# The last group of a two-level Winograd projection: another product is taken plainly and comes last

## The chip, the cores and the metric

The kernel runs on one core of a Trainium2 chip. Its time is the device time of one execution in microseconds (us); several executions are made, and the median counts. A profile is one further execution, recorded instruction by instruction. The engines of the core are named as the profile names them: PE is TensorE (matrix products; PEld is its loading of weights), DVE is VectorE (elementwise arithmetic), ACT is ScalarE (here copies, squares, and one of the two queues from which transfers are issued), POOL is GpSimd, and SP is SyncE, which issues most transfers. PSUM is the memory that TensorE writes its products into; it is taken in banks of 128 partitions by 512 fp32 numbers. All else on the chip lies in SBUF.

## The reference

An attention block without softmax, then a feed-forward block with two matrices multiplied element by element:

```python
kv  = np.einsum('bhsd,bhse->bhde', k, v)          # q, k, v: (8, 8, 576, 64)
out = np.einsum('bhsd,bhde->bhse', q, kv)
rms = np.sqrt(np.mean(out * out, axis=-1, keepdims=True) + 1e-06)
x   = (out / rms * g_norm)                        # turned to (4608, 512)
a = x @ w1                                        # w1, w2: (512, 1024)
b = x @ w2
h = a * b @ w3                                    # w3: (1024, 1024)
return (h @ w_out)                                # w_out: (1024, 512)
```

All is fp32. The weights come as 64-bit floats and are converted in the kernel.

## The kernel before, in words

**Folding.** `w3 @ w_out` is computed once, at the start, into `w3o_sb` (1024 by 512, held as 128 partitions x 8 chunks x 512). What is left of the feed-forward block is then `(x w1) * (x w2)`, and that times `w3o`.

**Groups.** The 4608 rows are worked on in nine groups of 512 rows. Eight are the first 512 rows of a batch each; the ninth collects the 64 rows that are left over of every batch. The order is 0 to 6, then the left-over rows, then batch 7. In a group, `gates` computes `ab = (x w1) * (x w2)` in four pieces `p`, and then the projection multiplies `ab` by `w3o`. Attention for the next batch is threaded between the pieces; the last two groups have none of it.

**Winograd products.** A product of two 2x2 block matrices A and B is made of seven block products instead of eight (Winograd's form of Strassen's algorithm). With sums s1, s2, s3, s4 of A's blocks and differences t1, t2, t3, t4 of B's blocks, the products are

- p1 = a11 b11, a12 b21, p5 = s1 t1, s2 t2, s4 b22, s3 t3, a22 t4;
- u2 = p1 + s2 t2, u3 = u2 + s3 t3;
- c11 = p1 + a12 b21, c12 = u2 + p5 + s4 b22, c22 = u3 + p5, c21 = u3 + a22 t4.

The sums over several products are partly made in PSUM (a product is added onto a bank that holds an earlier one), partly by VectorE out of a copy kept in SBUF.

**Two levels.** The projection of the first group uses this once (`project`). That of the other eight groups (`project_twice`) uses it twice: each of the seven block products ("sets" here) is itself made of seven products of a quarter of the size. The sets are numbered by what they multiply: 0 is a11 b11, 1 is s1 t1, 2 is s2 t2, 3 is s4 b22, 4 is s3 t3, 5 is a12 b21, 6 is a22 t4. For a set n,

- `sum_inner(n)` makes the inner sums of the A side on VectorE: four additions of 128x256, three into one of three buffers (`inner_sums[n % 3]`), and the last in place in the block itself;
- `load_b()` fetches the B side of the next set, made ready beforehand, from device memory into one of three stream buffers, on SP's queue or, for sets 3 and 5, on ScalarE's;
- `products(n, ps)` runs the seven small products (L898) into two PSUM banks, four in the first and three in the second; given banks `ps` of an earlier set it adds onto them, unless `new` is true, when the banks are begun afresh;
- `keep(name, ps)` copies both banks to SBUF on ScalarE (L909, L910), and `add(z, ps)` adds them onto such a copy on VectorE (L937, L938), one instruction a bank;
- `finish(z, half, j)` combines the seven parts of a block of the result and writes it to `o_sbs[half]`, four instructions (L919 to L922). For the last group it also stores the block (`store_block`), except where the block still lacks a term.

A block (half, j) is the result's c(half+1)(j+1): rows of one half, columns of one half.

**The last group** (`last`) doesn't run set 6. Its product a22 t4 is taken plainly instead, in `last_block`: eight matmuls of 128x256 (two halves `m` of the rows, four chunks) into one bank, the two halves side by side. VectorE then adds each half onto block (1,0), which `finish(z, 1, 0)` has left without that term, and two stores bring it out, one on SP's queue and one on ScalarE's. A matmul in fp32 leaves two records in the trace, so that a set of fourteen matmuls has 28 and the plain product 16.

**Preparing the B side.** `prepare_b`, threaded through the second group, makes the inner differences of the seven B blocks (in place for one of them) and writes all to `w3o_l2` in device memory: parts 0 to 6. Before any of it, it saves one block untransformed as part 7: this is what the plain product multiplies by. `load_b` reads part `n % 7` for the n-th load; the last load of all, `ALL_B - 1`, reads the first 1024 columns of part 7.

**Order.** TensorE's, POOL's and SP's instructions are issued in the order in which the program makes them; VectorE's too within `project_twice` (a manual schedule, L1123). Where a later instruction would write what an earlier one reads, or the other way round, a semaphore keeps them apart.

Of the kernel before, what the change touches and what calls it, by code (L numbers as in the profile page):

```python
# [21 lines left out]
def kernel(  # L22
# [32 lines left out]
    nc = tc.nc  # L55
    PSUM = bass.MemoryType.PSUM
    P = 128
# [24 lines left out]
    def bank(pool, tag):  # L82
        return pool.tile([P, 512], FP32, name=tag, tag=tag)
# [717 lines left out]
    def prepare_b():  # L801

        nc.sync.dma_start(
            out=w3o_l2[7, :, 0:1024].rearrange("p (f n) -> p f n", n=N), in_=b_blocks()[6]
        )
        for n, y in enumerate(b_blocks()):
            b11, b12, b21, b22 = (
                y[:, 2 * i:2 * i + 2, j * P:(j + 1) * P] for i in range(2) for j in range(2)
            )


            stage = w3o_sums[0].rearrange("p f n -> p (f n)") if n == 4 else (
                o_sbs[(n - n // 5) % 2].rearrange("p m n -> p (m n)")
            )
            stage = stage[:, 0:6 * P]
            t1, t2, t4 = (t.rearrange("p (c n) -> p c n", n=P) for t in (
                stage[:, i * 2 * P:(i + 1) * 2 * P] for i in range(3)
            ))
            nc.vector.tensor_sub(t1, b12, b11)
            nc.vector.tensor_sub(t2, b22, t1)  # L820
            nc.vector.tensor_sub(b12, b22, b12)
            nc.vector.tensor_sub(t4, b21, t2)
            nc.sync.dma_start(
                out=w3o_l2[n, :, 0:1024].rearrange("p (f n) -> p f n", n=N), in_=y
            )
            nc.sync.dma_start(out=w3o_l2[n, :, 1024:PART], in_=stage)
            yield
# [4 lines left out]
    def load_b():  # L832
        n = len(loaded_b)
        if n == ALL_B:
            return
        t = streams[n % len(streams)]

        queue = nc.scalar if n % 7 in (3, 5) else nc.sync
        if n + 1 < ALL_B:
            queue.dma_start(out=t, in_=w3o_l2[n % 7])  # L840
        else:
            t = t[:, 0:1024]
            queue.dma_start(out=t, in_=w3o_l2[7, :, 0:1024])
        loaded_b.append(t)

    inner = {}

    def sum_inner(n, between=lambda: None):

        s1, s2, s4 = ab_sums  # L850
        x = [ab[0][:, :, 0], s1, s2, s4, ab[0][:, :, 1], ab[1][:, :, 0], ab[1][:, :, 1]][n]
        a11, a12, a21, a22 = (
            x[:, 2 * j:2 * j + 2, i * P:(i + 1) * P] for i in range(2) for j in range(2)
        )
        s1, s2, s4 = inner_sums[n % 3]
        nc.vector.tensor_add(s1, a21, a22)
        nc.vector.tensor_sub(s2, s1, a11)
        nc.vector.tensor_sub(s4, a12, s2)
        between()
        nc.vector.tensor_sub(a21, a11, a21)  # L860
        inner[n] = [a11, a12, a22, s1, s2, s4, a21]

    def project_twice(T, last, ahead):
        def store(half):
            if T < B:
                rows = out[T * S:T * S + G, :].rearrange("(p j) f -> p j f", j=J)
                nc.sync.dma_start(out=rows[:, 2 * half:2 * half + 2, :], in_=o_sbs[half])
                return
            for m in range(2):
                for l in range(2):  # L870
                    b = 2 * (2 * half + m) + l
                    nc.sync.dma_start(
                        out=out[b * S + G:(b + 1) * S, :], in_=o_sbs[half][l * L:(l + 1) * L, m, :]
                    )

        def products(n, ps=None):

            new = ps is None or n == 5
            if ps is None:
                ps = [bank(ps_mm, "mm").rearrange("p (i n) -> p i n", n=P) for _ in range(2)]  # L880
            a11, a12, a22, s1, s2, s4, s3 = inner[n]
            w = loaded_b[7 * done[T] + n]
            b = w[:, 0:1024].rearrange("p (f n) -> p f n", n=N)
            b11, t3, b21, b22 = (
                b[:, 2 * i:2 * i + 2, j * P:(j + 1) * P] for i in range(2) for j in range(2)
            )
            t1, t2, t4 = (
                w[:, 1024 + 256 * i:1280 + 256 * i].rearrange("p (c n) -> p c n", n=P)
                for i in range(3)
            )  # L890
            seen = set()
            for place, x, y in (
                (0, a11, b11), (3, a12, b21), (1, a22, t4), (2, s1, t1), (6, s2, t2), (5, s4, b22),
                (4, s3, t3),
            ):
                to, i = ps[place // 4], place % 4
                for c in range(2):
                    nc.tensor.matmul(  # L898
                        to[:, i, :], lhsT=x[:, c, :], rhs=y[:, c, :],
                        start=new and place // 4 not in seen,  # L900
                        stop=(c == 1),
                        skip_group_check=True,
                    )
                    seen.add(place // 4)
            return ps

        def keep(name, ps):
            t = late_tile(name)
            nc.scalar.copy(t[:, 0:4], ps[0])  # L909
            nc.scalar.copy(t[:, 4:7], ps[1][:, 0:3])  # L910
            return t

        def finish(z, half, j):

            def wide(i):
                return z[:, i:i + 1].to_broadcast([P, 2, P])

            dst = o_sbs[half][:, :, j * N:(j + 1) * N].rearrange("p m (i n) -> p m i n", n=P)
            nc.vector.tensor_add(z[:, 6], z[:, 6], z[:, 0])  # L919
            nc.vector.tensor_add(z[:, 4:6], z[:, 4:6], wide(6))  # L920
            nc.vector.tensor_add(dst[:, 1], z[:, 1:3], wide(4))
            nc.vector.tensor_add(dst[:, 0], z[:, 3:6:2], z[:, 0:3:2])  # L922
            if not last:
                if j == 0:
                    store(half)
            elif (half, j) != (1, 0):
                store_block(half, j)

        def store_block(half, j, a=0, b=2, queue=nc.sync):
            rows = out[T * S:T * S + G, j * N:(j + 1) * N].rearrange("(p j) f -> p j f", j=J)  # L930
            queue.dma_start(
                out=rows[:, 2 * half + a:2 * half + b, :],
                in_=o_sbs[half][:, a:b, j * N:(j + 1) * N],
            )

        def add(z, ps):
            nc.vector.tensor_add(z[:, 0:4], ps[0], z[:, 0:4])  # L937
            nc.vector.tensor_add(z[:, 4:7], ps[1][:, 0:3], z[:, 4:7])  # L938

        done[T] = len(done)  # L940

        def last_block():

            a22, t4 = ab[1][:, :, 1], loaded_b[7 * done[T] + 6]
            t4 = t4.rearrange("p (f n) -> p f n", n=N)
            ps = bank(ps_mm, "mm").rearrange("p (m n) -> p m n", m=2)
            for m in range(2):
                for p in range(NF):
                    nc.tensor.matmul(
                        ps[:, m, :], lhsT=a22[:, p, m * P:(m + 1) * P], rhs=t4[:, p, :],  # L950
                        start=(m == 0 and p == 0), stop=(p == NF - 1), skip_group_check=True,
                    )
            for m in range(2):
                dst = o_sbs[1][:, m, 0:N]
                nc.vector.tensor_add(dst, dst, ps[:, m, :])
                store_block(1, 0, m, m + 1, nc.scalar if m else nc.sync)


        r1 = products(0)
        p1 = keep("p1", r1)  # L960
        load_b()
        sum_inner(2)
        for f in ahead:
            f()
        r2 = products(1)
        p5 = keep("p5", r2)
        load_b()
        sum_inner(3)
        products(2, r1)
        z = keep("u2", r1)  # L970
        load_b()
        sum_inner(4)
        products(3, r2)
        load_b()
        add(z, r2)
        sum_inner(5)
        finish(z, 0, 1)
        products(4, r1)
        if last:

            add(p5, r1)
        z = keep("u3", r1)
        load_b()
        if not last:
            sum_inner(6)
            nc.vector.tensor_add(p5, p5, z)
        finish(p5, 1, 1)
        if last:

            finish(z, 1, 0)  # L990
        products(5, r2)
        load_b()
        add(p1, r2)
        finish(p1, 0, 0)
        if last:
            last_block()
        else:
            products(6, r1)
            load_b()
            finish(keep("u4", r1), 1, 0)  # L1000
# [179 lines left out]
```

## Time and profile before

| | us |
|---|---|
| median of 5 runs | 772.15 |
| lowest and highest | 769.78, 772.92 |
| the profiled execution: time | 772.22 |
| the profiled execution: span, first to last instruction | 770.4 |
| last group: its projection begins on TensorE | 743.06 |
| TensorE's last matmul (L949) ends | 765.44 |
| VectorE's last addition (L955) ends | 766.84 |
| last store issued | 766.88 |

The granted TensorE clock is 0.998 of full speed over the span. The span is about 1.8 us shorter than the execution's own time; what lies around it is outside the profile. In the lists of instructions, a row has the start, the time taken, the engine, the line, the operation and its tiles, how many instructions were merged, and in brackets how long the engine idled before it and what ended that. `raw` is the pool in which `o_sbs`, `ab_sums` and one of the streams lie; `w3o_sb` holds the two other streams once the B side has been prepared; `mm` and `at` are the two pools of PSUM banks, five and three of them; `u` and `p` are copies made by `keep`.

VectorE's instructions in the last group, before the change, in order, by the starts in the trace: inner sums of set 4 (751.10), `add` of set 3 (754.50), inner sums of set 5 (756.31), `finish` of (0,1) (757.90), `add` of set 4 (759.35), `finish` of (1,1) (760.54), `finish` of (1,0) (762.00), `add` of set 5 (763.45), `finish` of (0,0) (764.64), the two plain additions (766.10).

### The profile page before, as it was taken

The numbers are of one execution on the slowest core, as the hardware profiler recorded it, in microseconds if no ns is written. First come the engines' busy times: TensorE is split into PE (matmuls) and PEld (weight loads), VectorE is DVE, ScalarE is ACT, GpSimd is POOL, SyncE is SP. The second block draws the span as 40 slices with busy tenths as digits, with TensorE's granted clock in tenths as the row PEclk, the third lists the DMA queues.
The fourth block names the chain that finished last, engine by engine and source line by source line (L and its number), as shares of the span: only waits on it lengthen the run. The fifth ranks groups of instructions, "written<-read, shape, count | busy, mean of one in ns | idle before, by whom it ended". The sixth has DMA issues, their size and how long they took to land.

```text
span 770.4 us, 14422 instructions
## 1 busy us (share of the span) xinstructions
PE 759.8 (99%) x5775; PEld 660.0 (86%) x5775; DVE 539.0 (70%) x1083; ACT 253.5 (33%) x487; POOL 134.6 (17%) x132
## 2 busy tenths in 40 slices
PE   8999999999999999999999999999999999999997
PEld 5455788888899889988998899889888998898897
DVE  6977999439978577756776776658665863594566
ACT  6777753213322232223213322232233222212221
POOL 0000000122611451133114501340154000000000
PEclk9999999999999999999999999999999999999999
DMA  9995641338997854873486648744741460074014
GB/s 318 331 337 178 215 140 40 83 95 253 331 288 263 227 111 138 269 201 101 132 284 170 131 144 281 171 110 148 269 70 42 160 230 0 1 244 146 1 55 171
DMA packets 132775, 132.55 MB, mean 172 GB/s; under 512 B 76644, under 2 KB 120676, under 8 KB 132708
## 3 DMA queue, kind: packets, MB, share of 16 engines
q1 hardware_dynamic: 130256, 116.81, 51.3%
q10 hardware_dynamic: 2452, 14.81, 5.6%
q8 instruction: 46, 0.75, 0.4%
q14 instruction: 21, 0.17, 0.1%
HBM read 100.27 MB, written 16.38 MB: 151 GB/s over the span
## 4 chain that ended last, share of the span: by engine, by line
PE 94%; DMA 4%; DVE 1%; ACT 0%; issue 0%; SPq 0%; DVEq 0%; ACTq 0%
PE mm L623 60%; PE mm L898 20%; PE mm L602 7%; PE at L332 3%; PE at L415 2%; DMA raw<-in_moe_w_out_dram 1%; DMA raw<-w3o_l 1%; DMA w3o_sb<-w3o_l 1%; PE at L589 1%; PE at L351 1%; DMA raw<-in_moe_w_dram 0%; PE at L448 0%; PE at L433 0%; DMA out_dram<-raw 0%; ACT ab L157 0%
## 5 line engine op out<-in xcount | busy, mean ns | idle before, releaser
L623 PE MATMUL mm<-xT,w_sb 128*128 128x256 f32 x768 | 176.2, 379 | 0.0
L623 PEld LDWEIGHTS mm<-xT,w_sb 128*128 128x128 f32 x768 | 145.5, 190 | 20.0 <-issue 0.5
L623 PE MATMUL mm<-xc,ws 128*128 128x256 f32 x576 | 130.2, 379 | 0.0
L623 PEld LDWEIGHTS mm<-xc,ws 128*128 128x128 f32 x576 | 109.4, 190 | 14.9
L762 DVE TENSOR_TENSOR c<-mm,u 128x512 f32<-128x512 f32 x36 | 24.9, 691 | 108.1 <-PE mm L623 108.1
L636 ACT COPY u<-mm 128x512 f32<-128x512 f32 x74 | 43.3, 586 | 138.7 <-PE mm L623 131.3
L636 ACT COPY p<-mm 128x512 f32<-128x512 f32 x74 | 43.4, 586 | 84.2 <-PE mm L623 82.2
L623 PE MATMUL mm<-xc,w_sb 128*128 128x256 f32 x288 | 69.3, 383 | 0.0
L898 PE MATMUL mm<-w3o_sb,raw 128*128 128x128 f32 x500 | 62.0, 275 | 0.1
L602 PE MATMUL mm<-chunks,ab 128*128 128x512 f32 x128 | 60.2, 601 | 1.8 <-DVE chunks L170 1.7
L623 PE MATMUL mm<-xT,ws 128*128 128x256 f32 x256 | 61.1, 381 | 0.0
L290 POOL COPY xT<-xn 128x1024 uint16<-128x1024 uint16 x26 | 31.8, 1251 | 163.9 <-DVE xn L393 163.6
L623 PEld LDWEIGHTS mm<-xc,w_sb 128*128 128x128 f32 x288 | 53.6, 190 | 7.8 <-ACT u L636 0.3
L898 PEld LDWEIGHTS mm<-w3o_sb,raw 128*128 128x128 f32 x500 | 58.9, 192 | 0.3 <-issue 0.3
L763 DVE TENSOR_TENSOR ab<-c 128x256 f32<-128x256 f32 x108 | 56.5, 524 | 3.0
L623 PEld LDWEIGHTS mm<-xT,ws 128*128 128x128 f32 x256 | 48.0, 190 | 6.6
L384 DVE TENSOR_REDUCE inv<-sq 128x8 f32<-128x512 f32 (+1 forms) x40 | 23.4, 626 | 36.6 <-ACT sq L383 36.6
L762 DVE TENSOR_TENSOR c<-p,u 128x512 f32<-128x512 f32 x36 | 27.6, 767 | 29.0 <-ACT u L636 28.9
L898 PE MATMUL mm<-w3o_sb,ab 128*128 128x128 f32 x336 | 43.9, 275 | 0.8 <-DMA w3o_sb<-w3o_l 0.8
L909 ACT COPY u<-mm 128x512 f32<-128x512 f32 x23 | 13.5, 586 | 88.6 <-DVE raw L922 53.5
L898 PEld LDWEIGHTS mm<-w3o_sb,ab 128*128 128x128 f32 x336 | 41.1, 192 | 1.3 <-issue 1.0
L602 PEld LDWEIGHTS mm<-chunks,ab 128*128 128x128 f32 x128 | 21.9, 190 | 22.8 <-issue 15.8
(158 smaller groups left out, 1139.5 us busy)
## 6 DMA issues: line engine op xcount, KB each, us to landing
w3o_sb<-w3o_l SPq DMA_DIRECT2D x26, 896.0 KB, 5.4
raw<-in_moe_w_dram SPq DMA_DIRECT2D x31, 512.0 KB, 7.0
raw<-w3o_l SPq DMA_DIRECT2D x13, 896.0 KB, 6.0
w3o_sb<-w3o_l ACTq DMA_DIRECT2D x11, 896.0 KB, 4.6
k_sb<-in_k_dram SPq DMA_DIRECT2D x32, 256.0 KB, 3.8
v_sb<-in_v_dram SPq DMA_DIRECT2D x32, 256.0 KB, 4.4
q_sb<-in_q_dram SPq DMA_DIRECT2D x32, 256.0 KB, 4.2
out_dram<-raw SPq DMA_DIRECT2D x14, 512.0 KB, 3.6
```

The source lines that it names most:

```text
L290: nc.gpsimd.tensor_copy(to, src.rearrange("p a n w -> p w a n"))
L332: nc.tensor.matmul(kv_ps[e * D:(e + 1) * D, r - rs[0], :], lhsT=k_sb[:, e, cols] if j < J else kl[:, 2 * r + e, :], rhs=v_sb[:, e, cols] i ...
L351: nc.tensor.transpose(qt_ps[:, e, i, :], q_sb[:, e, i * P:(i + 1) * P], ident)
L384: nc.vector.tensor_reduce(out=inv[:, i], in_=sq.rearrange("p (h d) -> p h d", d=D), axis=AX.X, op=ALU.add)
L415: nc.tensor.matmul(o_ps[l][tokens, n * D:(n + 1) * D], lhsT=qT[r][rows, e, i, tokens], rhs=kv_b[rows, e, r, :], start=True, stop=True,)
L602: nc.tensor.matmul(sums_ps[half][m], lhsT=w3T[half, c][:, m, :], rhs=chunks[:, c, 1, :], start=(c == 0), stop=(c == KF - 1),)
L623: nc.tensor.matmul(ps[:, u, :], lhsT=lhsT(a_name, u, c), rhs=rhs(b_name, c),  start=(u == 0 and c == 0 and to is None), stop=(c == chunks ...
L636: nc.scalar.copy(t, ps)
L762: nc.vector.tensor_add(c, one, two)
L763: nc.vector.tensor_mul(dst, c[:, 0, :], c[:, 1, :])
L898: nc.tensor.matmul(to[:, i, :], lhsT=x[:, c, :], rhs=y[:, c, :], start=new and place // 4 not in seen, stop=(c == 1), skip_group_check=True,)
L909: nc.scalar.copy(t[:, 0:4], ps[0])
```

## The change

For the last group alone, sets 5 and 6 change roles. Set 6 (a22 t4) is now run as a set of seven small products, in the place where set 5 stood; a12 b21, which was set 5, is taken plainly and comes last. So block (1,0) is complete with set 6, and block (0,0) is the one that waits for the plain product.

- `prepare_b` saves b21 as part 7 in place of t4. `load_b` reads part 6 for the last but one load and part 7 for the last.
- `sum_inner` gets an argument for the buffer: set 6's inner sums go to the buffer of place 5, and are made right after `products(3)` is issued. Right behind them VectorE runs `finish(p1, 0, 0)`, without a store: the block's part from p1 alone. Only then comes the `add` of set 3.
- `products(6, r2)` begins its banks afresh and takes load number 5 of the group. Behind it come `add(z, r2)` and `finish(z, 1, 0)`, which now stores block (1,0).
- `last_block` has a PSUM bank of the other pool (`at`) for each half of the rows. Each half's addition and store follow its four matmuls in the program; the addition is onto block (0,0).

The order of all other groups is as it was.

```diff
@@ prepare_b
-            out=w3o_l2[7, :, 0:1024].rearrange("p (f n) -> p f n", n=N), in_=b_blocks()[6]
+            out=w3o_l2[7, :, 0:1024].rearrange("p (f n) -> p f n", n=N), in_=b_blocks()[5]
@@ load_b
+        part = {ALL_B - 2: 6, ALL_B - 1: 7}.get(n, n % 7)
+
         queue = nc.scalar if n % 7 in (3, 5) else nc.sync
         if n + 1 < ALL_B:
-            queue.dma_start(out=t, in_=w3o_l2[n % 7])
+            queue.dma_start(out=t, in_=w3o_l2[part])
         else:
             t = t[:, 0:1024]
-            queue.dma_start(out=t, in_=w3o_l2[7, :, 0:1024])
+            queue.dma_start(out=t, in_=w3o_l2[part, :, 0:1024])
         loaded_b.append(t)
@@ sum_inner
-    def sum_inner(n, between=lambda: None):
+    def sum_inner(n, between=lambda: None, place=None):
...
-        s1, s2, s4 = inner_sums[n % 3]
+        s1, s2, s4 = inner_sums[(n if place is None else place) % 3]
@@ products
-            new = ps is None or n == 5
+            new = ps is None or n == 5 or last and n == 6
...
-            w = loaded_b[7 * done[T] + n]
+            w = loaded_b[7 * done[T] + (5 if last and n == 6 else n)]
@@ finish
-            elif (half, j) != (1, 0):
+            elif (half, j) != (0, 0):
                 store_block(half, j)
@@ last_block
-            a22, t4 = ab[1][:, :, 1], loaded_b[7 * done[T] + 6]
-            t4 = t4.rearrange("p (f n) -> p f n", n=N)
-            ps = bank(ps_mm, "mm").rearrange("p (m n) -> p m n", m=2)
+            a12, b21 = ab[1][:, :, 0], loaded_b[7 * done[T] + 6]
+            b21 = b21.rearrange("p (f n) -> p f n", n=N)
             for m in range(2):
+                ps = bank(ps_at, "at")[:, 0:N]
                 for p in range(NF):
                     nc.tensor.matmul(
-                        ps[:, m, :], lhsT=a22[:, p, m * P:(m + 1) * P], rhs=t4[:, p, :],
-                        start=(m == 0 and p == 0), stop=(p == NF - 1), skip_group_check=True,
+                        ps, lhsT=a12[:, p, m * P:(m + 1) * P], rhs=b21[:, p, :],
+                        start=(p == 0), stop=(p == NF - 1),
                     )
-            for m in range(2):
-                dst = o_sbs[1][:, m, 0:N]
-                nc.vector.tensor_add(dst, dst, ps[:, m, :])
-                store_block(1, 0, m, m + 1, nc.scalar if m else nc.sync)
+                dst = o_sbs[0][:, m, 0:N]
+                nc.vector.tensor_add(dst, dst, ps)
+                store_block(0, 0, m, m + 1, nc.scalar if m else nc.sync)
@@ the order of the group
         products(3, r2)
         load_b()
-        add(z, r2)
-        sum_inner(5)
+        if last:
+            sum_inner(6, place=5)
+
+            finish(p1, 0, 0)
+            add(z, r2)
+        else:
+            add(z, r2)
+            sum_inner(5)
         finish(z, 0, 1)
         products(4, r1)
...
         finish(p5, 1, 1)
+        products(6 if last else 5, r2)
+        load_b()
         if last:
-
+            add(z, r2)
             finish(z, 1, 0)
-        products(5, r2)
-        load_b()
-        add(p1, r2)
-        finish(p1, 0, 0)
-        if last:
             last_block()
         else:
+            add(p1, r2)
+            finish(p1, 0, 0)
             products(6, r1)
```

## The prediction

> **What bounds the kernel now.** I read the head of the page first, then its chain of waits, then the last thirty microseconds instruction by instruction, and last the DMA.
>
> ```profile
> span 770.4 us, 14422 instructions
> PE 759.8 (99%) x5775; PEld 660.0 (86%) x5775; DVE 539.0 (70%) x1083; ACT 253.5 (33%) x487; POOL 134.6 (17%) x132
> PE 94%; DMA 4%; DVE 1%; ACT 0%; issue 0%; SPq 0%; DVEq 0%; ACTq 0%
> ```
>
> TensorE is busy 99% of the span and makes 94% of the chain that ended last. VectorE (DVE) has 1% of it, some 8 us, and that is where this change works. The chain in order of time shows where:
>
> ```profile
> 743.22 12.52 PE mm L898 x112
> ...
> 755.84 0.56 DVE u L938
> ...
> 763.54 0.60 DVE p L937
> 764.14 0.48 DVE p L938
> ...
> 766.18 0.66 DVE raw L955 x2
> ```
>
> The chain leaves TensorE at 755.8 us and stays on VectorE to the end; the one DMA piece inside it, at 759.47, is a store that nobody computes on, for VectorE worked straight through it. The merged list of instructions shows the same stretch with its idle times in brackets:
>
> ```profile
> 754.50 0.69 DVE L937 TENSOR_TENSOR u<-mm,u 128x512 f32<-128x512 f32 x1 [1.59 <-PE mm L898]
> 755.57 1.50 PE L898 MATMUL mm<-raw,ab 128*128 128x128 f32 x12
> 755.84 0.56 DVE L938 TENSOR_TENSOR u<-mm,u 128x384 f32<-128x384 f32 x1 [0.65 <-PE mm L898]
> ...
> 761.82 3.62 PE L949 MATMUL mm<-w3o_sb,ab 128*128 128x256 f32 x16
> ...
> 766.10 0.74 DVE L955 TENSOR_TENSOR raw<-raw,mm 128x256 f32<-128x256 f32 x2
> 766.88 0.34 ACTq L931 DMA_DIRECT2D out_dram<-raw  x1
> ```
>
> VectorE idles 1.59 + 0.65 us, waiting for the fourth inner set of products, and after 755.84 shows no idle time any more. TensorE ends at 761.82 + 3.62 = 765.44, but the two last additions begin only at 766.10, because the last `add` and `finish` (763.45 to 766.10) stand ahead of them. So at the very end VectorE, not TensorE, is late. What follows the last addition is a store:
>
> ```profile
> out_dram<-raw SPq DMA_DIRECT2D x3, 256.0 KB, 2.2
> ...
> out_dram<-raw ACTq DMA_DIRECT2D x1, 128.0 KB, 2.4
> ```
>
> The last store is issued at 766.88 and lands 2.4 later, at 769.28; 1.12 us after that the span ends at 770.4.
>
> **What is removed and added.** In the last group nothing is added and nothing removed, by count. TensorE runs six inner sets of products and one plain product before and after. The chain's 112 records from 743.22 (four sets) make a set 28 records in 12.52 / 4 = 3.13 us; the plain product is 16 records, 3.62 us. VectorE has the same inner sums (four additions of 128x256 a set), the same four calls of `finish`, the same calls of `add` and the same two last additions. The loads are as many, as large and at the same places of the same queues; the output stores too. So TensorE's end stays at 765.44 unless something makes it wait.
>
> **What is moved.** Steps, from the distance between starts in the list: the inner sums of one set took 756.31 to 757.90, 1.59; a `finish` 760.54 to 762.00, 1.46; an `add` 763.45 to 764.64, 1.19, with its second half 0.60 after the first. The second half of an `add` starts 0.27 after the next set's first matmul (755.84 against 755.57), when TensorE has ended the set. VectorE's order after the change is then, from the end of the inner sums of set 4 (last one starts 752.49, next start 752.83):
> - inner sums of set 6, from 752.83 to 754.42, and the first `finish` (block 0,0 without its last product), to 755.88. Together 3.05 us; the idle 1.59 + 0.65 = 2.24 takes most of it. The first half of the following `add` had started at 754.50 there, so it moves back by 1.38, and ends at 755.88 + 1.19 = 757.07.
> - `finish` of block (0,1): to 758.53 (its store is issued 0.9 earlier than at 759.47).
> - `add` to p5: second half not before set 4's end, 758.69 + 0.27 = 758.96; first half 758.53, second 759.13, done 759.72. `finish` (1,1) to 761.18. ScalarE's copies of u3 follow that `add` as before (now about 759.3 to 760.3).
> - `add` of set 6 to u3: first half 761.18, second waits for the set's end, 761.82 + 0.27 = 762.09, done 762.68. `finish` (1,0) to 764.14 and its store.
> - first plain addition: its bank is complete at 761.82 + 1.81 = 763.63, VectorE is free at 764.14, done 764.55, store.
> - second: TensorE's end 765.44 + 0.10 (755.84 stands 0.10 behind the modelled end of the matmul before it: start 755.46 and 0.275 long) = 765.54, plus 0.41 for one L955 = 765.95; the store follows 0.04 later, as now (766.84 to 766.88): 765.99.
>
> So the last store is issued 766.88 - 765.99 = 0.89 earlier. VectorE is then free a whole microsecond (764.55 to 765.54) before the last product is; that is the cover for every error in this table, and behind it stand only the last addition and its store.
>
> **What lies behind the store.** Now the last three stores (256, 128 and 128 KB) are issued within 0.7 us and share the wires: the windows show 243, 343, 346, 336 and 44 GB/s from 767.0 to 769.0. After the change 384 KB are issued at about 764.2 and 764.6 and have moved, at that rate, by about 766.5; the last 128 KB go nearly alone. The trace has no lone 128 KB store. From above it is the 2.4 it has now; the nearest row, 256 KB alone (issue 759.47, landed 2.19 later, moving from about 760.4 to 761.25), less half of its 0.85 of movement gives 1.75 from below. I take 2.0, between them. Landing 767.99, plus 1.12: span 769.1, a gain of 1.3 (0.9 to 1.55).
>
> A rule that speaks against part of this: the Trainium skill, "DMA: Bandwidth & Descriptors", section "Anatomy of one DMA — SWDGE (gpsimd) path", fits a transfer at about 2.0 us fixed plus bytes over 436 GB/s. By it, as an estimate for a path that this kernel's stores don't take, 128 KB would land in 2.3 and the gain would be 1.0; 256 KB would take 2.6, and the row above shows 2.2, so I stay with the row.
>
> **Separate banks.** The first addition is drawn forward to 764.14, while TensorE still works on the second half of the product. In the trace the two halves of an `add`, one PSUM bank each, start apart (754.50 and 755.84), the first while TensorE goes on in the other bank; the plain product gets two such banks. Should the addition nevertheless wait for both halves, it would stand 0.37 ahead of the last one: gain 0.9 instead of 1.3. TensorE finds both banks free: their pool was last used by the attention part, long before this group. The Trainium skill, "PSUM — Partial Sum Buffer", section "PSUM bank collisions raise a hardware error", wants two engines kept apart by bank, not by address; by it the product in one bank, as it was, would give the 0.9. The trace has the same habit: ScalarE's first copy of u3 waits 6.96 us, until VectorE's read of the same bank has ended.
>
> **Waits that the order adds.** Behind the first half of the first `add` stand the stores of (0,1) and (1,1), both earlier than now. TensorE's set in the sixth place writes the bank that this `add` reads: free at 757.07, wanted at 758.69, cover 1.6 (was 2.3). Its inner sums are ready at 754.42 instead of 757.98, its operand arrives by the same load (ScalarE's queue, 752.70). The inner-sum buffer is the one of set 2, whose matmuls end at 752.43, before the write at 752.83.
>
> **The copy at the start.** The block that is saved untransformed is now b21, out of `w3o_sb`, instead of t4. The old one took 0.61 us on SP's queue at 177.2 and landed in 3.8; the four transfers of the same size out of `w3o_sb` took 0.43 to 1.64. So SP changes by -0.2 to +1.0, taken as 0: the loads behind it are for matmuls of the next batch, 12 us later and more (loads from 181.76, used at 200.1), and TensorE is unbroken there. The rewriting of b21 that must wait for it starts at 198.5, 17 us after it landed.
>
> **The sum.** Span 770.4 - 1.3. The profiled execution took 772.22, 1.8 more than its span, and lies 0.07 above the median of 772.15: 772.22 - 1.3 = **770.9 us**, 0.17% less. About 0.3%, 2.3 us, is what a measurement of this kernel can tell from no change (five runs lie from 769.78 to 772.92), so the forecast is "within 0.3%".
>
> **Rivals.**
> 1. *The end hardly moves.* VectorE isn't early enough, or the last store takes 2.4 and the tail grows. Against: a microsecond of room. It would come if VectorE's steps ran 1 us later than my table. Gain 0 to 0.5: 771.9.
> 2. *More than 2.3 us of gain.* The tail would have to shrink too. The least that I can build is 1.55; another 0.8 would have to come from the 1.12 behind the landing, with fewer stores open, or from a median that falls low, as one of five runs did (769.78). 769.5.
> 3. *Slower: VectorE is held at the start of the first doubled group.* VectorE rewrites part of `w3o_sb` at 169.29, and the saving copy, now out of the same tile and issued first in the program, goes out at 177.2 and lands at 181.0. If the order were kept by the whole tile, the rewriting would stand until 181.0, and VectorE's next eviction, now at 176.99, would come 7.3 us later (11.7 less the 4.38 that VectorE idles before 174.42). Of TensorE's five PSUM banks I take two as free, 1.73 us a product there (168.04 to 169.77), so it stands 7.3 - 3.5 = 3.8: 772.2 + 3.8 - 1.3 = 774.7. It decides from 3.6 us of stall. Against: VectorE already rewrites one quarter at 190.09 while the copy of another, earlier in the program, is issued only at 193.35; order is kept by parts, and b21 lies apart from what is rewritten first.
>
> **Chances.** Forecast 0.71, rival 1 0.11, rival 2 0.12, rival 3 0.06. Faster by over 0.3% 0.12, within 0.82, slower 0.06. The forecast's own terms give 770.6 to 771.3; the runs scatter by more, so the range is 769.2 to 772.7, with rival 1 inside.
>
> **What would show it.** Right: L623 and L898 unchanged in count and mean, TensorE unbroken from 743 to 765.4; no `add` or `finish` after the last matmul, one 128x256 addition only, with VectorE idle about a microsecond before it, released by TensorE; the last store issued at about 766.0 and landing in 1.75 to 2.4. Wrong: an idle gap of TensorE ahead of the sixth set or the plain product; the first plain addition later than 765; VectorE idle on a DMA near 169 us; a span outside 768.8 to 769.6.

## The result, and the profile after

| | before | after |
|---|---|---|
| median, us | 770.68 (86 runs) | 769.30 (48 runs) |
| lowest and highest | 769.19, 773.52 | 767.38, 773.24 |
| ratio, 95% interval | | 0.9982 [0.9976, 0.9987] |
| profiled execution: time, span | 772.22, 770.4 | 768.31, 766.5 |
| last group's projection begins on TensorE | 743.06 | 740.69 |
| from there to the end of the span ("the tail") | 27.34 | 25.81 |

The change makes the kernel 0.18% faster, 1.4 us, which many runs can tell though it is less than the 0.3% named in the prediction. The two profiles differ by far more, 3.9 us of span. Only 1.53 of that lies in the tail; the other 2.37 lie ahead of the last projection, where both kernels do the same work. The experiments take this up first.

The head of the page, after the change:

```profile
span 766.5 us, 14426 instructions
PE 759.3 (99%) x5775; PEld 659.8 (86%) x5775; DVE 541.7 (71%) x1083; ACT 253.8 (33%) x487; POOL 134.4 (18%) x132
```

The end of the chain of waits in order of time (start, us, what; L900 is what L898 was, L951 what L949 was, L956 what L955 was):

```profile
740.85 18.76 PE mm L900 x168
759.61 3.47 PE at L951 x16
763.10 0.42 DVE raw L956
```

Matmuls and VectorE instructions are as many as before. The chain now stays on TensorE to its last matmul, through all six sets (168 records) and the plain product; in this stretch VectorE has one addition in it where it had 11 us. The list of instructions of the same stretch, after:

```profile
750.46 0.42 DVE L858 TENSOR_TENSOR inner_sums<-ab 128x256 f32<-128x256 f32 x1
...
752.19 0.28 DVE L921 TENSOR_TENSOR p<-p 128x128 f32<-128x128 f32 x1
...
753.65 0.68 DVE L939 TENSOR_TENSOR u<-mm,u 128x512 f32<-128x512 f32 x1
754.25 0.55 DVE L940 TENSOR_TENSOR u<-mm,u 128x384 f32<-128x384 f32 x1
...
759.45 3.62 PE L951 MATMUL at<-w3o_sb,ab 128*128 128x256 f32 x16
...
761.44 0.42 DVE L924 TENSOR_TENSOR raw<-u 128x256 f32<-128x256 f32 x1
761.77 0.41 DVE L956 TENSOR_TENSOR raw<-raw,at 128x256 f32<-128x256 f32 x1
763.10 0.42 DVE L956 TENSOR_TENSOR raw<-raw,at 128x256 f32<-128x256 f32 x1 [0.92 <-PE at L951]
763.56 0.34 ACTq L933 DMA_DIRECT2D out_dram<-raw  x1
```

The brackets have changed sides. The `add` of set 3 (L939, L940) no longer shows idle time before it, because the inner sums of set 6 (from 750.46) and one `finish` (from 752.19) now fill it; the idle time, 0.92 us, stands before the very last addition, and TensorE ended it. The first half of the plain product was added at 761.77, while TensorE worked on the second until 759.45 + 3.62 = 763.07. The windows give TensorE 22.38 us of work from 740.69 to 766.5: exactly 740.69 to 763.07, without a gap. The stores, by size and time from issue to landing:

```profile
out_dram<-raw SPq DMA_DIRECT2D x3, 256.0 KB, 2.2
...
out_dram<-raw ACTq DMA_DIRECT2D x1, 128.0 KB, 1.9
```

The last one lands in 1.9 us where it took 2.4.

### The profile page after: what moved, and what is told of

Its sections match the earlier page's. It is cut to its first block, busy times and chain, and to the rows that moved or that the text cites. A ratio compares the mean times of both kernels' runs of the same rounds, so it can differ in the third digit from the quotient of the medians.

```text
span 766.5 us, 14426 instructions
## 1 busy us (share of the span) xinstructions
PE 759.3 (99%) x5775; PEld 659.8 (86%) x5775; DVE 541.7 (71%) x1083; ACT 253.8 (33%) x487; POOL 134.4 (18%) x132
## 4 chain that ended last, share of the span: by engine, by line
PE 96%; DVE 2%; DMA 1%; ACT 1%; issue 0%; SPq 0%; DVEq 0%; ACTq 0%
PE mm L623 60%; PE mm L900 21%; PE mm L602 7%; PE at L332 3%; PE at L415 2%; PE at L589 1%; DMA raw<-in_moe_w_out_dram 1%; PE at L351 1%; PE at L951 0%; PE at L448 0%; PE at L433 0%; DVE ab L160 0%; DVE xc L666 0%; ACT ab L157 0%; DVE raw L677 0%
## 5 line engine op out<-in xcount | busy, mean ns | idle before, releaser
L900 PE MATMUL mm<-w3o_sb,raw 128*128 128x128 f32 x500 | 62.3, 275 | 0.2 <-DVE raw L858 0.2
L763 DVE TENSOR_TENSOR ab<-c 128x256 f32<-128x256 f32 x108 | 59.9, 555 | 3.0
L900 PEld LDWEIGHTS mm<-w3o_sb,raw 128*128 128x128 f32 x500 | 59.0, 192 | 0.5 <-DVE raw L858 0.4
L900 PE MATMUL mm<-w3o_sb,ab 128*128 128x128 f32 x336 | 43.8, 275 | 0.0
L900 PEld LDWEIGHTS mm<-w3o_sb,ab 128*128 128x128 f32 x336 | 41.0, 192 | 0.4
```

The costliest lines, as they stand in the source:

```text
L763: nc.vector.tensor_mul(dst, c[:, 0, :], c[:, 1, :])
L900: nc.tensor.matmul(to[:, i, :], lhsT=x[:, c, :], rhs=y[:, c, :], start=new and place // 4 not in seen, stop=(c == 1), skip_group_check=True,)
```

## The experiments

All times of a tail are taken from one profile each: the first matmul of the last projection, TensorE's last matmul, the last store, the end of the span. TensorE's last matmul ends 22.37 or 22.38 after the projection's begin in all of them but one (22.43, told there), so that whatever changes, changes behind it.

| kernel | last store issued, after the begin | tail | ratio to before, 95% interval |
|---|---|---|---|
| before | 23.82 | 27.34 | |
| before, again | 23.82 | 27.41 | 0.9998 [0.9985, 1.0012] |
| changed | 22.87 | 25.81 | 0.9982 [0.9976, 0.9987] |
| changed, again | 22.87 | 25.84 | 0.9982 [0.9967, 0.9996] |
| swap and banks alone | 24.01 | 27.06 | 1.0002 [0.9987, 1.0017] |
| inner sums early, finish late | 23.51 | 26.49 | |
| one bank | 23.20 | 26.18 | 0.9983 [0.9971, 0.9995] |
| one store of 256 KB | 22.86 | 26.23 | 0.9977 [0.9965, 0.999] |
| before, with two banks | 23.81 | 27.39 | |
| two more on VectorE | 22.87 | 25.87 | |
| five more on VectorE | 24.03 | 27.00 | |
| last half in two quarters | 22.79 | 25.43 | 0.9971 [0.9955, 0.9987] |

The page gives a span to a tenth, so a tail is good to about 0.05 us and a difference of two tails to 0.1; the issue of the last store is known to a hundredth. The two repeated tails agree within this, 0.07 and 0.03. Of every other kernel there is one tail. The ratio of a dozen runs is uncertain by more than 0.1%, about 1 us. So the tails carry the verdicts on steps of a few tenths, and the ratios only say that nothing larger was missed.

**Is the gain in the tail alone?** Both kernels once more, without any edit.

> The kernel before, once more. The tail (first matmul of the last group's projection to the end of the span) was 27.34 us before the change (743.06 to 770.4) and 25.81 after it (740.69 to 766.5), 1.53 less; but the spans differ by 3.9, since the last projection itself began 2.37 earlier. Theory A (the gain lies in the tail alone, the 2.37 is chance, mostly two late loads of a B block ahead of projections): tail 27.3 again, ratio 0.999 to 1.001, and the projection begins anywhere from 740.5 to 743.5, with stalls at other places or none. Theory B (the change also removes stalls ahead of the last group): the projection begins near 743 again, with TensorE standing on the same two loads.

> The changed kernel once more. Theory A (gain in the tail alone): tail 25.8, ratio 0.998 to 0.9985, its last projection beginning anywhere from 740.5 to 743.5. Theory B (stalls ahead of the last group removed too): beginning at 740.7 again.

The tails came out at 27.41 and 25.84. The begins, 743.79 and 740.46, lie just outside theory A's bounds on either side, and taken alone they look like theory B. What speaks against B is, first, where TensorE stood. The late loads in the chain of the repeated run of before:

```profile
228.04 7.29 DMA w3o_sb<-w3o_l
...
539.13 6.76 DMA w3o_sb<-w3o_l
```

In the first profile of before:

```profile
538.10 6.92 DMA w3o_sb<-w3o_l
...
681.29 6.96 DMA raw<-w3o_l
```

And in the changed kernel with VectorE's old order, a run of the next experiment:

```profile
462.83 6.74 DMA w3o_sb<-w3o_l
...
681.28 6.75 DMA raw<-w3o_l
```

The load at 681 was late there too, in a kernel that has the whole change but for VectorE's order behind 743, so the change doesn't remove it. Two more variants of the changed kernel stood on a load: the late `finish`, below, at 680.63 (6.47 us), and the one with quarters at 464.93 (6.63 us), which began its last projection at 743.87, later than before. What two late loads cost can be read from where each projection begins. In the first profiles of before and of the changed kernel the fifth two-level projection began at 525.40 and 525.27, the sixth at 601.42 and 600.22, the seventh at 671.65 and 670.46, the last at 743.06 and 740.69: 1.07 and 1.18 arise in the two stretches with a late load, 2.25 of the 2.37. (The repeated run of before stood a third time, 0.80 us ahead of 689.12, where the profile names VectorE and no load.)

Second, the runs that were only timed. The shortest span of a run of before was 767.1, that of a run of the changed kernel 765.6; less their tails both began at 739.8. And the medians differ by 1.38, not 3.9; the interval of the ratio allows 1.0 to 1.85. Nor is it the clock: 0.998 over the span of before and 1.000 after the change, but in before it is 1.00 in every stretch up to 767.8, and lower only behind the last matmul. Theory A stands: the 2.37 are late loads that come and go, with the change's products as without, and the tail's 1.53 is all that the runs show the change to do.

**Whose part is it?** First with VectorE's old order, so that only the swap of the products and the banks remain:

```diff
-            sum_inner(6, place=5)
-
-            finish(p1, 0, 0)
             add(z, r2)
+            sum_inner(6, place=5)
...
             finish(z, 1, 0)
+            finish(p1, 0, 0)
             last_block()
```

> The changed kernel with VectorE's old order: inner sums of the sixth place after the add of set 3, and the finish of block (0,0) right ahead of the plain additions. Swap of the products and two banks stay. Theory (the gain comes from VectorE's work drawn into its idle time): VectorE is late as before, additions 23.0 us after the projection's begin, tail 27.3, ratio 0.999 to 1.001. Rival (the swap or the banks bring it): tail 25.8 to 26.4, ratio 0.998.

The ratio is that of no change, and VectorE is late as before. Its last instructions:

```profile
765.55 0.42 DVE L924 TENSOR_TENSOR raw<-p 128x256 f32<-128x256 f32 x1
766.07 0.75 DVE L956 TENSOR_TENSOR raw<-raw,at 128x256 f32<-128x256 f32 x2
...
766.85 0.34 ACTq L933 DMA_DIRECT2D out_dram<-raw  x1
```

The begin was 742.84, so the additions start at 23.23 instead of 23.04. The tail missed the expected 27.3 by 0.3 all the same: 27.06. The last store was issued later (24.01) but the span ended only 3.05 behind it, where it took 3.52 before. With the roles swapped, the 256 KB store of the block that was ready early (now (1,0)) goes out a whole `finish` ahead of the two last ones, and the last 128 KB land in 1.9 instead of 2.4 here too. The 256 KB were issued at 764.54 here, 2.31 ahead of the last store, and at 766.21 in the kernel before, 0.67 ahead. VectorE itself is 0.19 later than before; so a part of the gain, 0.28 on balance, is the order of the stores and not VectorE's time. That the order makes the store land sooner is read from these issue times; no run moved that store alone.

Then only the `finish` put back late, the inner sums early:

```diff
             sum_inner(6, place=5)
 
-            finish(p1, 0, 0)
             add(z, r2)
...
             finish(z, 1, 0)
+            finish(p1, 0, 0)
             last_block()
```

> The changed kernel with only the finish of block (0,0) put back right ahead of the plain additions; the inner sums stay early. Theory: 1.59 of inner sums fit the idle time, 1.46 of finish come back on the path and VectorE is the last again: the last addition ends 0.45 later than in the changed kernel, tail 26.4 (between 26.2 and 26.6). If the finish alone were the gain: 27.3; if the inner sums alone: 25.8.

26.49, as expected. But the last addition ends 0.65 later than in the changed kernel, not 0.45: the 0.2 more is as much as the plain additions start later here too, 0.52 behind the last instruction of `finish` instead of 0.33. From 27.34 the way down is then: swap 0.28, inner sums into the idle time 0.57, `finish` into the idle time 0.68, together 1.53, each step good to 0.1. The issue of the last store, the sharper measure, moves by 0.50 and 0.64 in the last two.

**Separate banks.** The plain product in one bank, otherwise as changed:

```diff
-            for m in range(2):
-                ps = bank(ps_at, "at")[:, 0:N]
+            ps = bank(ps_at, "at").rearrange("p (m n) -> p m n", m=2)
+            for m in range(2):
                 for p in range(NF):
                     nc.tensor.matmul(
-                        ps, lhsT=a12[:, p, m * P:(m + 1) * P], rhs=b21[:, p, :],
-                        start=(p == 0), stop=(p == NF - 1),
+                        ps[:, m, :], lhsT=a12[:, p, m * P:(m + 1) * P], rhs=b21[:, p, :],
+                        start=(m == 0 and p == 0), stop=(p == NF - 1), skip_group_check=True,
                     )
+            for m in range(2):
                 dst = o_sbs[0][:, m, 0:N]
-                nc.vector.tensor_add(dst, dst, ps)
+                nc.vector.tensor_add(dst, dst, ps[:, m, :])
                 store_block(0, 0, m, m + 1, nc.scalar if m else nc.sync)
```

> The changed kernel with the plain product in one bank, its two additions after all sixteen records. Theory: both additions wait for TensorE's end, the second ends 0.37 later and the two half stores go out together: tail 26.2 to 26.6 against 25.8, ratio 0.9986. Rival (an addition can start on its half while TensorE fills the other half of the bank): 25.8, the first addition a microsecond and more before TensorE's end.

```profile
760.08 3.62 PE L951 MATMUL at<-w3o_sb,ab 128*128 128x256 f32 x16
...
763.73 0.75 DVE L957 TENSOR_TENSOR raw<-raw,at 128x256 f32<-128x256 f32 x2 [1.25 <-PE at L951]
764.52 0.34 ACTq L933 DMA_DIRECT2D out_dram<-raw  x1
```

Both additions start after TensorE's end (763.70), merged into one row. They were also written after all the matmuls here, so the run shows what one bank with that order costs, 0.37, and doesn't show what VectorE would have done had the first addition been allowed sooner. The rival is not settled beyond that. Banks alone, in the kernel before:

```diff
             for m in range(2):
+                ps = bank(ps_at, "at")[:, 0:N]
                 for p in range(NF):
                     nc.tensor.matmul(
-                        ps[:, m, :], lhsT=a22[:, p, m * P:(m + 1) * P], rhs=t4[:, p, :],
-                        start=(m == 0 and p == 0), stop=(p == NF - 1), skip_group_check=True,
+                        ps, lhsT=a22[:, p, m * P:(m + 1) * P], rhs=t4[:, p, :],
+                        start=(p == 0), stop=(p == NF - 1),
                     )
-            for m in range(2):
                 dst = o_sbs[1][:, m, 0:N]
-                nc.vector.tensor_add(dst, dst, ps[:, m, :])
+                nc.vector.tensor_add(dst, dst, ps)
```

> The kernel before with two banks for its plain product and each half's addition and store after its matmuls, nothing else. Theory: VectorE is late there whatever the banks, so tail 27.3. Rival (banks are a gain by themselves): 26.9.

27.39. Two banks are worth 0.37 where VectorE has time to use them, and nothing where it hasn't. So of the 0.68 that the early `finish` brings, about half needs the second bank as well.

**The last store.** Both halves in one store:

```diff
                 dst = o_sbs[0][:, m, 0:N]
                 nc.vector.tensor_add(dst, dst, ps)
-                store_block(0, 0, m, m + 1, nc.scalar if m else nc.sync)
+            store_block(0, 0, 0, 2, nc.scalar)
```

> The changed kernel with block (0,0) stored whole, 256 KB at once on ScalarE's queue, after the second addition. Theory (part of the gain is that the last store is small and alone: 128 KB landed in 1.9 us instead of 2.4): it lands in 2.2 to 2.4, tail 26.1 to 26.4. Rival (landing does not hang on the size): 1.9, tail 25.8.

It was issued at the same place (22.86), landed in 2.2, and the tail is 26.23, within the theory. How much is still to be moved counts, not only when it is issued. The ratio can't show this step; its interval holds the changed kernel's.

**Is the idle microsecond cover?** Extra subtractions on a free buffer, two and five, which add no result:

```diff
             finish(z, 1, 0)
+            s1, s2, s4 = inner_sums[0]
+            for _ in range(2):
+                nc.vector.tensor_sub(s1, s2, s4)
             last_block()
```

> The changed kernel with two subtractions of 128x256 more on VectorE (on a free buffer) ahead of the plain additions. Theory (0.92 us of idle time there is pure cover): 0.7 to 0.8 us more work, tail 25.8 unchanged, idle time down to 0.1 to 0.2. Rival (VectorE is still on the path): tail 26.5.

> The same with five subtractions more: 1.8 us, 0.9 beyond the cover. Theory: no idle time of VectorE left, last addition 0.9 later, tail 26.7 to 27.0 (the last stores come closer together). Rival (tail bound by something else): 25.8.

With five:

```profile
761.58 2.25 DVE L1002 TENSOR_TENSOR raw<-raw 128x256 f32<-128x256 f32 x5
...
763.75 0.74 DVE L956 TENSOR_TENSOR raw<-raw,at 128x256 f32<-128x256 f32 x2
764.53 0.34 ACTq L933 DMA_DIRECT2D out_dram<-raw  x1
```

Two more cost nothing: the last store is issued at 22.87 as without them. Five take 2.17 (761.58 to 763.75), more than the expected 1.8, push both additions behind TensorE's end (762.88) and the store to 24.03: 1.16 later, and the tail to 27.0. So VectorE had 2.17 - 1.16 = 1.0 to spare, about the 0.92 of idle time, and no more.

**A version beyond.** The second half of the plain product in two quarters by columns, in banks of their own, so that the last addition is half as large and the last store 64 KB:

```diff
-            for m in range(2):
-                ps = bank(ps_at, "at")[:, 0:N]
+            for k, (m, c, w) in enumerate(((0, 0, N), (1, 0, P), (1, P, P))):
+                ps = bank(ps_at, "at")[:, 0:w]
                 for p in range(NF):
                     nc.tensor.matmul(
-                        ps, lhsT=a12[:, p, m * P:(m + 1) * P], rhs=b21[:, p, :],
+                        ps, lhsT=a12[:, p, m * P:(m + 1) * P], rhs=b21[:, p, c:c + w],
                         start=(p == 0), stop=(p == NF - 1),
                     )
-                dst = o_sbs[0][:, m, 0:N]
+                dst = o_sbs[0][:, m, c:c + w]
                 nc.vector.tensor_add(dst, dst, ps)
-                store_block(0, 0, m, m + 1, nc.scalar if m else nc.sync)
+                rows = out[T * S:T * S + G, c:c + w].rearrange("(p j) f -> p j f", j=J)
+                (nc.scalar if k == 2 else nc.sync).dma_start(
+                    out=rows[:, m:m + 1, :], in_=o_sbs[0][:, m:m + 1, c:c + w]
+                )
```

> The changed kernel with the second half of the plain product split by columns: two products of 128 columns in banks of their own, each added and stored by itself, so that one addition of 128x128 and a store of 64 KB (512 B a row) stand behind the last matmul. Theory: last addition 0.13 shorter, store 0.1 to 0.2 sooner landed, TensorE 0.06 longer: tail 25.5 to 25.7 against 25.8, ratio 0.998. Rival (rows of 512 B cost more than the smaller size saves): 26.0 and more.

```profile
766.34 0.29 DVE L956 TENSOR_TENSOR raw<-raw,at 128x128 f32<-128x128 f32 x1 [0.61 <-PE at L951]
766.66 0.34 ACTq L958 DMA_DIRECT2D out_dram<-raw  x1
```

That is the end of its list of instructions; its last store, with size and time to landing, is

```profile
out_dram<-raw ACTq DMA_DIRECT2D x1, 64.0 KB, 1.6
```

TensorE ends 0.05 later (22.43), the addition is 0.13 shorter, the store lands in 1.6 instead of 1.9. The tail is 25.43, 0.38 below the changed kernel's and a little under the range expected; rows of 512 B cost nothing visible. Beside the changed kernel on the same chip the medians were 768.99 and 769.13, and both ratios' intervals overlap: it is ahead of the kernel before clear of noise, ahead of the changed kernel by its tail alone, which is one profile.

## Why the prediction was right

- **VectorE is late at the end, TensorE not.** Right, and the main reason. With VectorE's order put back most of the gain went (tail 27.06; ratio 1.0002, which can't tell the 0.28 that is left from none). With it, the chain stays on TensorE up to the one last addition.
- **The table of steps.** It put the first plain addition 21.08 behind the projection's begin (764.14 - 743.06) and the second at 22.48; measured 21.08 and 22.41. The last store was put at 22.93, measured 22.87, 0.95 earlier than before where 0.89 was worked out. The steps taken from distances between starts of the same instructions, not from their durations, made this close: a 128x256 addition is 0.41 to 0.43 long, but the next one starts 0.33 to 0.53 after it. One step was wrong: the inner sums were put at 1.59 and took 1.73 (750.46 to 752.19). It did no harm, because the second half of the last `add` waits for TensorE's set all the same: it was put at 19.03 behind the begin and started there (759.72). The exact 21.08 owes that to the wait, and not to the table.
- **A microsecond of cover.** Right: 0.92 idle, and two more subtractions were free.
- **Landing of the last store.** Taken as 2.0 between 1.75 and 2.4; it was 1.9; what follows it is 1.0 to 1.1 in both, as far as tenths tell. The gain in the tail is 1.53, at the far end of the 0.9 to 1.55 given. The Trainium skill's fit ("DMA: Bandwidth & Descriptors", section "Anatomy of one DMA — SWDGE (gpsimd) path") had given an estimate of 2.3; the last stores, which don't take that path, were quicker than its estimates at 64, 128 and 256 KB, and slower only in the kernel before, where 128 KB behind 384 KB took 2.4.
- **Where that part comes from** was put half right. The prediction had the last store alone because VectorE is early; the run with VectorE's old order has it at 1.9 too, because the swap lets the large store go first; another 128 KB issued 0.33 ahead of it did not keep it from 1.9.
- **Separate banks.** The fallback was given as a gain of 0.9 instead of 1.3, 0.4 less; one bank cost 0.37.
- **The copy at the start.** Right: b21 was saved in 0.61 on SP's queue at 176.74, landing 3.7 later, and VectorE's rewriting of `w3o_sb` ran at 168.77, ahead of it. Rival 3 fell on that.
- **The size.** 1.3 us of gain forecast, 1.38 between the medians, 0.17% against 0.18%, so "within 0.3%" held. The time itself, 770.9, is 1.6 above the 769.30: it was counted from a profiled execution of 772.22 and five runs, and 86 runs put the kernel before at 770.68. That is the base, not a step of the change. That 769.30 still lies inside the stated 769.2 to 772.7, by 0.1, is luck: what was foreseen is the size of the change, not the time. Rival 2's 769.5 is nearer for the same reason, a low median of the runs; the gain over 2.3 us that it stood for did not come.
- **One test of its own was badly chosen.** "a span outside 768.8 to 769.6" was to show the forecast wrong, and the span was 766.5. A span from one profile carries what happens ahead of the last group, and the last projection began anywhere from 740.23 to 743.87 in the twelve profiles; the tail, which doesn't, was forecast as 26.05 (769.11 - 743.06) and was 25.81.

## What to carry to other kernels

Work on an engine that idles early and is late at the end is worth moving into its idle time, and the distances between starts in the trace say to within 0.2 us here what that brings. Behind the last matmul, make what is left small: one small addition and one small store, with everything large issued ahead of it. When a change touches one stage, compare that stage from a fixed point in both profiles, since two spans can differ by more than the change for reasons that both kernels share.

## What the runs showed that was not expected

- The start-to-start distance on VectorE varies with what the next instruction reads. An addition onto a block other than the one just written starts 0.33 behind the last `finish` instruction (761.44 to 761.77); onto the block just written, 0.52 (765.55 to 766.07, swap alone; 764.12 to 764.64 with the late `finish`). That dependence is a likely reason and was not tried by itself. It isn't the whole: the same first two steps of the inner sums take 0.45 and 0.46 in one place (756.31 to 757.22, before) and 0.52 and 0.53 in another (750.46 to 751.51, after).
- The last stores land in 1.6 (64 KB), 1.9 (128 KB) and 2.2 us (256 KB): 0.3 a step, though the steps of size are 64 and 128 KB. What else is under way counts too: 128 KB took 2.4 behind 384 KB issued within 0.7 us (before).
- The loads of the B blocks, which land in about 5 us by their median, are now and then so late that TensorE stands about 1 us, in some executions twice and in others never; that makes much of the difference between profiles.
